# Maxima over partitions by a DMA transpose or by TensorE, in a fused local attention and feed-forward kernel

## Chip, core and metric

The kernel runs on one core of a Trainium2 chip. The metric is the device time of one execution in microseconds. Of three timed executions of the kernel before, the median was 618.79 us (614.6 to 619.58).

The engines are named as the profile names them: PE is TensorE's matmuls and PEld its weight loads, DVE is VectorE, ACT is ScalarE, POOL is GpSimd, and SP is the engine on whose queue this kernel issues all its DMAs. Each engine runs its instructions in the order in which they were recorded; one that waits holds back all behind it.

## What is computed

Attention over 4 batches, 8 heads, 768 positions and 64 channels, in which each position sees the keys less than 16 positions away and the 24 block summaries of its batch; then, on the same 3072 tokens of 512 channels, a feed-forward layer of width 2048. Cut from the reference:

```python
k_sum = k.reshape(B, H, nb, 32, D).max(axis=3)
v_sum = v.reshape(B, H, nb, 32, D).mean(axis=3)
scores_l = where(|i - j| < 16, scale * q @ k.T, -1e9)
scores_s = scale * q @ k_sum.T + log(32)
a = softmax(concat([scores_l, scores_s]))
x = a @ concat([v, v_sum])          # heads side by side: 3072 x 512
h = x @ w_in
out = (h * sigmoid(h)) @ w_out
```

## The kernel before, in words

**Precision sets the structure.** PE multiplies float16 here: a float32 operand is split into a high and a low half, and three products replace one. For that an operand is first scaled by a power of two, which is taken from the largest magnitude of the whole tensor. So before a batch's data can be split, a maximum (or a sum of magnitudes) that lies spread over the 128 partitions has to become one number that stands in every partition. `all_max` (L427) does that, eight times in the program: for the queries and keys of batches 1 to 3 (two columns, called by `job_scale`), for the values of batches 0 to 3 (one column, called by `v_scale`), and for the two weight matrices (two columns, called by `w_scale`). It writes the columns to DRAM (`sd`, L430), reads them back as one row spread to all partitions (`vms`, L431), and DVE reduces that row in each partition (L432). Five or six tiny DVE operations behind it make the scales (L441 to L446 for values: `sc`, `vsc`; L407 to L412 for queries and keys: `qc`, `qsc`; L813 to L817 for weights: `wc`, `ws`).

**Stages.** Batch 0 and the feed-forward of its first chunk of 256 tokens run in float32 (PE lines L626, L630, L688 and L727 for attention, L850 and L863 for the feed-forward) while the 16 MB of weights arrive (L771) and are decoded (ACT L785 and L789, DVE L791 and L792; the last gives the column maxima `wm`, and L810 reduces them to `wx`). Once `ws` is known, the weights are split in place (ACT L805, DVE L807). From there the feed-forward of the chunks 1 to 11 runs in float16, with L853 and L866 as its first and second product up to chunk 5, and L941 and L980 (fewer products, by sums of quarters) from chunk 6. The attention of the batches 1 to 3 is woven in two chunks ahead of its use: scores on PE (L623), a minimum with mask on DVE (L659), the exponential on ACT (L662), the split of the probabilities on DVE (L706) and their transposition by DMA (L709), then the product with the values (L742). Values of a batch need their scale before they are split (ACT L561, DVE L563) and written to DRAM. The three staging buffers `raw` are shared by all loads; `vR` is a transposed copy of the values that is loaded for their means and maxima (DVE L460, L462).

**What sets the order.** Nobody wrote the order by hand. The class `Plan` holds every operation with the engines it may run on, an assumed cost, its reads and writes by key and a priority. It places the operations on the engines by assumed times and latencies, forwards and backwards several times, and then records the instructions in order of their planned start. The assumed cost is the number in `plan.op({"dve": 140}, ...)`; an assumed DMA latency is added. The priorities contain the constants of the table `TUNE`. For `all_max` the plan assumes 600 and 450 ns for the two DMAs, beside their latencies. The plan also puts in idle matmuls (L337) where PE has nothing to do at the beginning.

Of the kernel before, what the change touches and what calls it, by code (L numbers as in the profile page):

```python
# [10 lines left out]
F32 = mybir.dt.float32  # L11
F32R = mybir.dt.float32r
F16 = mybir.dt.float16
U32 = mybir.dt.uint32
U16 = mybir.dt.uint16
AF = mybir.ActivationFunctionType
ALU = mybir.AluOpType
# [215 lines left out]
def local_attn_ffn(ctx: ExitStack, tc: tile.TileContext, qkT, qP, qF, kF, v, vR, vP, w, out):  # L233
# [23 lines left out]
    ident = const.tile([P, P], F32, name="ident")  # L257
    make_identity(nc, ident)

    sums = const.tile([P, BLK + 4 * NTILE - 4], F32, name="sums")  # L260
# [44 lines left out]
    md_t = [far.tile([NB, 2, DM], F16, name=f"md{i}") for i in range(B - 1)]  # L305
    sd_t = [far.tile([P, 2], F32, name=f"sd{i}") for i in range(2 * B)]
    vmf_t = const.tile([P, 4, P], F16, name="vmf")
# [27 lines left out]

    unit = ident.bitcast(mybir.dt.bfloat16)
    plan = Plan(tc, lambda: nc.tensor.matmul(out=bank[0][:, :2 * P], lhsT=unit[:, :P], rhs=unit, start=True, stop=True))  # L337
# [88 lines left out]

    def all_max(out, in_, r, w, prio):  # L427
        i, n = nxt("sd", 2 * B), in_.shape[1]
        flat, row = sd_t[i].rearrange("p n -> (p n)")[:n * P], vms_t[:, :n * P]
        plan.op({"dma": 600}, lambda e: nc.sync.dma_start(out=flat.rearrange("(p n) -> p n", n=n), in_=in_), r=r, w=[("sd", i)], prio=prio)  # L430
        plan.op({"dma": 450}, lambda e: nc.sync.dma_start(out=row, in_=flat.unsqueeze(0).to_broadcast([P, n * P])), r=[("sd", i)], w=[("vms", 0)], prio=prio)  # L431
        plan.op({"dve": 65 + 133 * n}, lambda e: nc.vector.tensor_reduce(out=out, in_=row.rearrange("q (p n) -> q n p", n=n), axis=AX.X, op=ALU.max), r=[("vms", 0)], w=w, prio=prio, port=())  # L432

# [3 lines left out]
    def v_scale(b, prio):  # L437
        vs = vsc_t[b % 2]
        all_max(sc2[:, 0:1], am_t[:, 7:8], ["am4"], ["sc2"], prio)
        steps = (  # L440
# [368 lines left out]
    def w_scale(prio):  # L809
        plan.op({"dve": 80}, lambda e: nc.vector.tensor_reduce(out=wx_t, in_=wm_t, axis=AX.X, op=ALU.max), r=[("wm", f, kind) for f in range(NFT) for kind in range(2)], w=["wx"], prio=prio)  # L810
        all_max(wc[:, 0:2], wx_t, ["wx"], ["wc"], prio)
        steps = (
            lambda e: nc.vector.tensor_scalar(out=wc[:, 2:4], in0=wc[:, 0:2], scalar1=1e-30, scalar2=None, op0=ALU.max),  # L813
            lambda e: nc.vector.tensor_scalar(out=wc[:, 0:2].bitcast(U32), in0=wc[:, 2:4].bitcast(U32), scalar1=0x7F800000, scalar2=None, op0=ALU.bitwise_and),
            lambda e: nc.vector.tensor_scalar(out=ws_t[:, 2:4], in0=wc[:, 0:2], scalar1=2.0 ** -12, scalar2=None, op0=ALU.mult),
            lambda e: nc.vector.reciprocal(out=ws_t[:, 0:2], in_=ws_t[:, 2:4]),
            lambda e: nc.vector.scalar_tensor_tensor(out=ws_t[:, 3:4], in0=ws_t[:, 2:3], scalar=1.0 / SHRINK, in1=ws_t[:, 3:4], op0=ALU.mult, op1=ALU.mult))  # L817
        for i, step in enumerate(steps):
            plan.op({"dve": 70}, step, w=["wc"] + (["ws"] if i > 1 else []), prio=prio)
# [348 lines left out]

TUNE = dict(quad=-30.75, vd=-11.0, ws=-845.5, s0=3027.0, wp=623.75, wm=55.75, km=703.75, w_dma=27.5, w_dec=-2.75, a0=490.0, a1=-2168.0, d1=201.25, span=75.25, post=3599.25, ffn2=753.0, jc0=-1061.5, jc1=716.0, jx0=-191.25, jx1=1364.5, vs=765.0, qk=-243.25, k=-423.0, v=1879.25, v0=-41.25, out=1280.75, first=65.75)

# [60 lines left out]
```

## Time and profile before

| | before |
|---|---|
| median of three executions | 618.79 us |
| profiled execution, its own time | 619.0 us |
| its span, first to last instruction | 617.2 us |
| mean granted clock of PE | 0.977 |
| PE busy | 580.0 us, 94% |
| PEld busy | 440.7 us, 71% |
| DVE busy | 470.3 us, 76% |
| ACT busy | 369.8 us, 60% |
| POOL busy | 170.4 us, 28% |
| HBM traffic | 119 GB/s over the span |

How to read it: the profile comes from one execution, whose own time is 619.0 us; the span is 1.8 us less. Busy times are the share in which an engine had an instruction under way. A granted clock of 1.00 is PE's 2.4 GHz, and 0.50 is 1.2 GHz; a stretch between them has had both.

### The profile page before, as it was taken

What the parts mean: (1) busy time and instruction counts of PE and PEld (TensorE: products, weight loads), DVE (VectorE), ACT (ScalarE), POOL (GpSimd) and SP (SyncE); (2) the same over time, 40 slices, a digit from 0 to 9 for tenths busy, and PEclk for the clock granted to TensorE, in tenths of its full rate; (3) what the DMA queues carried; (4) which work ended last, traced back from release to release, by engine and by line L of the source; (5) the groups of instructions that cost most, each with busy time, mean ns of one, the idle gap of its engine ahead of it and who ended that gap; (6) DMA issues with size and microseconds to landing.
All of it is one profiled execution on the core that took longest, in us unless ns stands there. A gap on an engine that the chain in (4) does not pass through costs nothing.

```text
span 617.2 us, 15861 instructions
## 1 busy us (share of the span) xinstructions
PE 580.0 (94%) x6235; PEld 440.7 (71%) x6235; DVE 470.3 (76%) x1244; ACT 369.8 (60%) x906; POOL 170.4 (28%) x318
## 2 busy tenths in 40 slices
PE   8988988996899998896999999999899999999997
PEld 5765645664566765563667688888688888888885
DVE  6986869885969585985789765886887988665655
ACT  4886929952847662843767674653567566544332
POOL 4230103200111022313322122452444554442220
PEclk9998999999899999897999999999799999999999
DMA  8998734331586666545665566244473722220001
GB/s 323 418 329 296 294 74 154 96 97 55 140 233 177 179 150 70 148 96 106 181 202 143 129 126 109 83 139 66 100 217 70 164 78 43 44 70 2 35 1 36
DMA packets 67698, 84.42 MB, mean 137 GB/s; under 512 B 44887, under 2 KB 46311, under 8 KB 65831
## 3 DMA queue, kind: packets, MB, share of 16 engines
q1 hardware_dynamic: 67622, 83.41, 49.1%
q8 instruction: 49, 0.80, 0.6%
q14 instruction: 27, 0.21, 0.2%
HBM read 62.39 MB, written 11.16 MB: 119 GB/s over the span
## 4 chain that ended last, share of the span: by engine, by line
PE 50%; DMA 27%; DVE 15%; ACT 5%; issue 2%; POOL 0%; SPq 0%; DVEq 0%; ACTq 0%
PE bank L941 15%; PE bank L980 13%; PE bank L866 9%; PE bank L853 8%; DMA sd<-am 7%; DMA vms<-sd 5%; DMA wr<-in_w_dram 3%; DMA raw<-in_vR_dram 2%; DMA wr<-in_v_dram 2%; PE bank L742 2%; DMA out_dram<-raw 2%; DVE e L659 1%; PE bank L623 1%; DMA sd<-qm 1%; DVE wr L807 1%
## 5 line engine op out<-in xcount | busy, mean ns | idle before, releaser
L941 PE MATMUL bank<-x,wr 128*128 128x256 f16 x1152 | 134.8, 273 | 0.0
L965 POOL TENSOR_TENSOR wr<-wr 128x128 f32<-128x128 f32 x160 | 88.2, 568 | 146.8 <-DVE wr L957 67.1
L941 PEld LDWEIGHTS <-wr 128*128 128x128 f16 x1152 | 112.5, 98 | 14.4
L980 PE MATMUL bank<-wr 128*128 128x256 f16 x987 | 119.3, 276 | 3.6 <-DVE sc L442 2.0
L853 PE MATMUL bank<-x,wr 128*128 128x256 f16 x960 | 112.2, 273 | 0.0
L980 PEld LDWEIGHTS <-wr 128*128 128x128 f16 x987 | 96.5, 99 | 17.2 <-DVE sc L442 2.3
L853 PEld LDWEIGHTS <-wr 128*128 128x128 f16 x960 | 93.7, 98 | 19.8 <-issue 0.9
L866 PE MATMUL bank<-wr 128*128 128x512 f16 x384 | 93.3, 390 | 9.3 <-DVE sc L441 4.9
L662 ACT ACTIVATE e<-e,mx 128x120 f32<-128x120 f32 x192 | 73.0, 382 | 26.1 <-DVE mx L659 23.7
L866 PEld LDWEIGHTS <-wr 128*128 128x128 f16 x384 | 36.9, 100 | 49.7 <-DVE sc L441 5.4
L675 POOL TENSOR_SCALAR first<-e,sum 128x120 f16<-128x120 f32 x54 | 24.5, 464 | 120.8 <-ACT e L662 29.4
L956 ACT ACTIVATE wr<-bank,th 128x512 f32<-128x512 f32 x47 | 32.0, 682 | 36.6 <-PE bank L941 36.4
L957 DVE SCALAR_TENSOR_TENSOR wr<-wr,bank 128x512 f32<-128x512 f32 x47 | 32.0, 682 | 27.3 <-ACT wr L956 27.3
L706 DVE SCALAR_TENSOR_TENSOR first<-e,sum,first 128x120 f16<-128x120 f32 x144 | 46.5, 375 | 0.0
L968 DVE SCALAR_TENSOR_TENSOR wr<-wr 128x512 f16<-128x512 f32 x47 | 33.7, 716 | 16.6 <-ACT wr L967 16.5
L967 ACT ACTIVATE wr<-wr 128x512 f16<-128x512 f32 x47 | 29.3, 623 | 26.4 <-POOL wr L965 26.3
L878 ACT ACTIVATE wr<-bank,th 128x512 f32<-128x512 f32 x32 | 21.8, 681 | 34.5 <-PE bank L853 34.3
L659 DVE CUSTOM_DVE_ANT_0 e<-bank,masks,qsc 128x120 f32<-128x120 f32 x144 | 41.1, 334 | 1.6 <-PE bank L623 1.6
L961 ACT ACTIVATE wr<-wr 128x384 f16<-128x384 f32 x47 | 24.4, 520 | 28.7 <-DVE wr L957 28.5
L246 POOL TENSOR_TENSOR wr<-wr 128x256 f32<-128x256 f32 x32 | 26.5, 846 | 36.9 <-DVE wr L926 30.7
L662 ACT ACTIVATION_READ_ACCUMULATOR e<-e,mx 128x1 f32 x192 | 36.1, 188 | 0.0
L962 DVE SCALAR_TENSOR_TENSOR wr<-wr 128x384 f16<-128x384 f32 x47 | 31.1, 662 | 4.7 <-ACT wr L961 3.8
(155 smaller groups left out, 861.5 us busy)
## 6 DMA issues: line engine op xcount, KB each, us to landing
wr<-in_w_dram SPq DMA_DIRECT2D x14, 1024.0 KB
raw<-in_qkT_dram SPq DMA_DIRECT2D x18, 576.0 KB
out_dram<-raw SPq DMA_DIRECT2D x23, 256.0 KB
first<-vd SPq DMA_DIRECT2D x30, 192.0 KB
raw<-in_kF_dram SPq DMA_DIRECT2D x12, 384.0 KB
raw<-in_qF_dram SPq DMA_DIRECT2D x9, 512.0 KB
raw<-in_vR_dram SPq DMA_DIRECT2D x12, 384.0 KB
raw<-in_vP_dram SPq DMA_DIRECT2D x9, 512.0 KB
```

The source lines that it names most:

```text
L659: plan.op({"dve": 262 if b else 206}, lambda e, i=i, j=j, et=et, mx=mx: nc.vector.tensor_tensor_reduce(out=et[:, i, :], in0=sc[j][:, i, :N ...
L662: plan.op({"act": 385}, lambda e, i=i, j=j, et=et, mx=mx: nc.scalar.activation(out=et[:, i, :], in_=et[:, i, :], func=AF.Exp, scale=-1.0, ...
L706: nc.vector.scalar_tensor_tensor(out=pt[:, i, P:P + NKEY], in0=et[:, i, :], scalar=su4[:, 2 * j + i:2 * j + i + 1], in1=pt[:, i, :NKEY], o ...
L853: nc.tensor.matmul(out=o, lhsT=wip[:, part, ct * P:(ct + 1) * P], rhs=x[:, ct, :], start=(ct == 0 and q == 0), stop=(ct == NCT - 1 and q = ...
L866: nc.tensor.matmul(out=bank[ob[u]][:, cs], lhsT=g[:, rows], rhs=wop[:, part, cs], start=(begins and q == 0), stop=(stops and q == 2))
L941: nc.tensor.matmul(out=h[:, at * CH:at * CH + CH], lhsT=wip[:, p, ct * P:(ct + 1) * P], rhs=x[:, ct, :], start=(ct == 0 and q == 0), stop= ...
L956: plan.op({"act": 573}, lambda e: nc.scalar.activation(out=t, in_=h, func=AF.Tanh, scale=th[:, 0:1]), r=bk(k) + [("th", b % 2), "areas"], ...
L957: plan.op({"dve": 604}, lambda e: nc.vector.scalar_tensor_tensor(out=t, in0=t, scalar=1.0, in1=h, op0=ALU.add, op1=ALU.mult), r=bk(k), w=t ...
L962: plan.op({"dve": 470}, lambda e: nc.vector.scalar_tensor_tensor(out=ld, in0=src, scalar=SHRINK, in1=hd, op0=ALU.mult, op1=ALU.subtract), ...
L965: plan.op({"pool": 470, "dve": 210}, lambda e, m=m, x=x, y=y, op=op: eng[e].tensor_tensor(out=sm[:, m], in0=x, in1=y, op=op), r=tks, w=[(" ...
L968: plan.op({"dve": 610}, lambda e: nc.vector.scalar_tensor_tensor(out=ls, in0=sf, scalar=SHRINK, in1=hs, op0=ALU.mult, op1=ALU.subtract), r ...
L980: nc.tensor.matmul(out=acc_of(c, m)[0], lhsT=x[:, left[m]], rhs=right[m](p), start=(opens and q == 0 and m in (1, 4, 2, 7)), stop=(closes ...
```

## The change

`all_max` gets two new forms, and the form over DRAM goes away together with its buffers `sd`.

For the queries, keys and values of the batches 1 to 3, DVE reads only the upper 16 bits of each float32, as bfloat16, and spreads each partition's value over 128 columns (L448, a copy inside `vms`). One DMA transpose turns that block (L449), so that every partition then holds all 128 values in a row, and DVE reduces them (L450). The scales use the exponent alone, which the upper 16 bits hold.

For the values of batch 0 and for the weights (`near`), PE transposes the column or columns to one row in PSUM (L438), DVE reduces the row on one partition (L441), a matmul with a row of ones spreads the result to 128 partitions (L442), and DVE copies it out of PSUM (L443).

The table `TUNE` is replaced as a whole, so priorities change everywhere and the plan orders all engines anew. The arithmetic of everything else is what it was. Lines after L257 move by 4, and lines behind `all_max` by 18: L741 to L760 in the new kernel are L723 to L742 in the old.

```diff
+    ones = const.tile([1, P], F32, name="ones")
+    nc.vector.memset(ones, 1.0)
+    row_t = const.tile([1, 2], F32, name="row")
...
-    sd_t = [far.tile([P, 2], F32, name=f"sd{i}") for i in range(2 * B)]
...
-    def all_max(out, in_, r, w, prio):
-        i, n = nxt("sd", 2 * B), in_.shape[1]
-        flat, row = sd_t[i].rearrange("p n -> (p n)")[:n * P], vms_t[:, :n * P]
-        plan.op({"dma": 600}, lambda e: nc.sync.dma_start(out=flat.rearrange("(p n) -> p n", n=n), in_=in_), r=r, w=[("sd", i)], prio=prio)
-        plan.op({"dma": 450}, lambda e: nc.sync.dma_start(out=row, in_=flat.unsqueeze(0).to_broadcast([P, n * P])), r=[("sd", i)], w=[("vms", 0)], prio=prio)
-        plan.op({"dve": 65 + 133 * n}, lambda e: nc.vector.tensor_reduce(out=out, in_=row.rearrange("q (p n) -> q n p", n=n), axis=AX.X, op=ALU.max), r=[("vms", 0)], w=w, prio=prio, port=())
+    def all_max(out, in_, r, w, prio, near=False):
+        n = in_.shape[1]
+        if near:
+            k = sbank()
+            row, spread = row_t[:, :n], bank[k][:, 2 * P:2 * P + n]
+
+            def turn(e):
+                for j in range(n):
+                    nc.tensor.transpose(out=bank[k][:1, j * P:(j + 1) * P], in_=in_[:, j:j + 1], identity=ident)
+
+            plan.op({"pe": 110 * n}, turn, r=r, w=bk(k), prio=prio, cols=128 * n)
+            plan.op({"dve": 65 + 133 * n}, lambda e: nc.vector.tensor_reduce(out=row, in_=bank[k][:1, :n * P].rearrange("o (a p) -> o a p", a=n), axis=AX.X, op=ALU.max), r=bk(k), w=["row"], prio=prio)
+            plan.op({"pe": 110}, lambda e: nc.tensor.matmul(out=spread, lhsT=ones, rhs=row, start=True, stop=True), r=["row"], w=bk(k), prio=prio, cols=1)
+            plan.op({"dve": 67}, lambda e: nc.vector.tensor_copy(out=out, in_=spread), r=bk(k), w=w, prio=prio)
+            return
+        top = in_.bitcast(BF16).rearrange("p (n i) -> p n i", i=2)[:, :, 1:].to_broadcast([P, n, P])
+        two = vms_t.bitcast(BF16)
+        here, there = (two[:, i * DM:i * DM + n * P].rearrange("p (n q) -> p n q", n=n) for i in range(2))
+        plan.op({"dve": 65 + 133 * n}, lambda e: nc.vector.tensor_copy(out=here, in_=top), r=r, w=[("vms", 0)], prio=prio)
+        plan.op({"dma": 1290}, lambda e: nc.sync.dma_start_transpose(out=there, in_=here.rearrange("p n q -> p (n q)")), r=[("vms", 0)], w=["tops"], prio=prio)
+        plan.op({"dve": 65 + 133 * n}, lambda e: nc.vector.tensor_reduce(out=out, in_=there, axis=AX.X, op=ALU.max), r=["tops"], w=w, prio=prio, port=())
...
-        all_max(sc2[:, 0:1], am_t[:, 7:8], ["am4"], ["sc2"], prio)
+        all_max(sc2[:, 0:1], am_t[:, 7:8], ["am4"], ["sc2"], prio, b == 0)
...
-        all_max(wc[:, 0:2], wx_t, ["wx"], ["wc"], prio)
+        all_max(wc[:, 0:2], wx_t, ["wx"], ["wc"], prio, True)
...
-TUNE = dict(quad=-30.75, vd=-11.0, ws=-845.5, s0=3027.0, wp=623.75, wm=55.75, km=703.75, w_dma=27.5, w_dec=-2.75, a0=490.0, a1=-2168.0, d1=201.25, span=75.25, post=3599.25, ffn2=753.0, jc0=-1061.5, jc1=716.0, jx0=-191.25, jx1=1364.5, vs=765.0, qk=-243.25, k=-423.0, v=1879.25, v0=-41.25, out=1280.75, first=65.75)
+TUNE = dict(quad=-1617.75, vd=-16.25, ws=-11.25, s0=-8.0, wp=1561.25, wm=184.25, km=10.25, w_dma=-1358.75, w_dec=-8.0, a0=-982.0, a1=-827.75, d1=698.0, span=86.25, post=3268.5, ffn2=759.5, jc0=-207.25, jc1=-485.5, jx0=-32.75, jx1=2269.75, vs=1653.25, qk=572.0, k=-650.75, v=1762.5, v0=301.75, out=-105.5, first=53.0)
```

How the order moves is shown at three places. The first is SP's queue while the weights are loaded and the scale of batch 0's values is made (`am` is the column of maxima, `in_w` the weights, `in_v` values, `in_qP` queries). In the kernel before:

```order
L527 DMA wr<-in_v_dram 128x1024 x2
L771 DMA wr<-in_w_dram 128x2048
L430 DMA sd_135<-am 128x1
L771 DMA wr<-in_w_dram 128x2048
L431 DMA vms<-sd_135 128x128
L486 DMA second<-in_qP_dram 128x512
L771 DMA wr<-in_w_dram 128x2048 x6
```

And SP's queue at that place in the changed kernel:

```order
L789 DMA wr<-in_w_dram 128x1024 x3
L789 DMA wr<-in_w_dram 128x2048 x6
L504 DMA second<-in_qP_dram 128x512
L789 DMA wr<-in_w_dram 128x2048 x4
L545 DMA wr<-in_v_dram 128x1024 x2
L789 DMA wr<-in_w_dram 128x2048 x3
```

The two DMAs of the maximum are gone from between the weight loads. The second place is DVE at the scale of batch 1's values, ahead of and behind the reduction that ends the round trip. In the kernel before:

```order
L760 SCALAR_TENSOR_TENSOR x_183<-bank_188,vsc_157,x_183 128x4x128
L497 SCALAR_TENSOR_TENSOR second<-raw_118,qsc_150,second 128x512
L882 SCALAR_TENSOR_TENSOR work<-work 128x512
L500 SCALAR_TENSOR_TENSOR second<-raw_118,qsc_150,second 128x4x160
L807 SCALAR_TENSOR_TENSOR wr<-wr,ws 128x2x512
L460 TENSOR_REDUCE vm<-raw_120 128x24
L659 ISA e_175,mx_169<-bank_191,masks,qsc_150 128x120
L659 ISA mx_169 128x1
L432 TENSOR_REDUCE sc_156<-vms 128x1
L879 SCALAR_TENSOR_TENSOR work<-work,bank_186 128x512
L659 ISA e_175,mx_169<-bank_191,masks,qsc_150 128x120
L659 ISA mx_169 128x1
```

And DVE there in the changed kernel:

```order
L448 COPY vms<-am 128x128
L518 SCALAR_TENSOR_TENSOR second<-raw_121,qsc_145,second 128x4x160
L778 SCALAR_TENSOR_TENSOR x_178<-bank_183,vsc_152,x_178 128x4x128
L478 TENSOR_REDUCE vm<-raw_123 128x24
L897 SCALAR_TENSOR_TENSOR work<-work,bank_181 128x512
L450 TENSOR_REDUCE sc_151<-vms 128x1
L900 SCALAR_TENSOR_TENSOR work<-work 128x512
L459 TENSOR_SCALAR sc_151<-sc_151 128x1
L677 ISA e_170,mx_164<-bank_186,masks,qsc_145 128x120
L677 ISA mx_164 128x1
```

Four operations now stand between the copy that starts the exchange and the reduction that ends it. The third place is SP's queue around the same scale (`in_vR` are the values for the maxima, `in_vP` those to be split). In the kernel before:

```order
L459 DMA raw_120<-in_vR_dram 128x768
L494 DMA raw_118<-in_qkT_dram 128x1152
L430 DMA sd_138<-am 128x1
L431 DMA vms<-sd_138 128x128
L560 DMA raw_118<-in_vP_dram 128x1024
L560 DMA raw_120<-in_vP_dram 128x1024
```

And in the changed kernel:

```order
L449 DMA_TRANSPOSE vms<-vms 128x2x128
L477 DMA raw_121<-in_vR_dram 128x768
L512 DMA raw_121<-in_qkT_dram 128x1152
L477 DMA raw_123<-in_vR_dram 128x768
L449 DMA_TRANSPOSE vms<-vms 128x1x128
L578 DMA raw_121<-in_vP_dram 128x1024
L578 DMA raw_123<-in_vP_dram 128x1024
```

The transposes stand where the pairs stood, and the loads of `in_vP` still follow; the transpose for the queries and keys is here too, with two of the four loads of `in_vR` behind it.

## Rows read from the trace of the kernel before

**Rows 1.** The page's first part: busy time, share of the span, instructions.
```profile
PE 580.0 (94%) x6235; PEld 440.7 (71%) x6235; DVE 470.3 (76%) x1244; ACT 369.8 (60%) x906; POOL 170.4 (28%) x318
```

**Rows 2.** PE's waits: line, whom it waited for, us in total, times, longest.
```profile
PE bank L623 <- DVE mx L659: 6.9, 2, 6.7
PE bank L866 <- DVE sc L441: 4.9, 1, 4.9
PE bank L866 <- ACT wr L881: 4.4, 1, 4.4
PE bank L626 <- DVE sc L441: 2.2, 1, 2.2
PE bank L980 <- DVE sc L442: 2.0, 1, 2.0
```

**Rows 3.** Timeline of DVE: start, us, operation, idle before and its end.
```profile
153.48 0.29 DVE L432 TENSOR_REDUCE sc<-vms 128x1 f32<-128x128 f32 x1 [7.04 <-DMA vms<-sd]
283.37 0.28 DVE L432 TENSOR_REDUCE sc<-vms 128x1 f32<-128x128 f32 x1 [8.44 <-DMA vms<-sd]
433.50 0.29 DVE L432 TENSOR_REDUCE sc<-vms 128x1 f32<-128x128 f32 x1 [6.84 <-DMA vms<-sd]
```

**Rows 4.** The chain that ended last, in order of time: start, us, what.
```profile
81.89 4.52 DMA sd<-wx
86.43 4.18 DMA vms<-sd
...
269.17 8.45 DMA sd<-am
277.64 5.71 DMA vms<-sd
```

**Rows 5.** Stretches: us, busy PE, PEld, DVE, ACT, POOL, PE's granted clock, DMA share, GB/s.
```profile
40.00:47.00 7.00, 5.35 (x23) 3.16 (x21) 4.93 (x11) 5.02 (x12) 2.46 (x6) 1.00 0.72 189
47.00:52.00 5.00, 3.38 (x12) 1.82 (x10) 1.09 (x2) 3.00 (x5) 0.00 (x0) 1.00 0.78 82
50.00:60.00 10.00, 7.78 (x82) 5.30 (x81) 7.81 (x29) 5.20 (x10) 0.00 (x0) 0.83 1.01 374
80.00:95.00 15.00, 13.04 (x97) 7.26 (x96) 9.50 (x19) 5.83 (x10) 0.00 (x0) 1.00 0.47 122
150.00:160.00 10.00, 3.93 (x56) 2.27 (x57) 6.20 (x31) 5.61 (x20) 1.57 (x4) 0.66 0.28 111
280.00:290.00 10.00, 5.68 (x22) 2.72 (x23) 6.21 (x22) 3.85 (x6) 2.55 (x6) 0.66 0.55 129
430.00:440.00 10.00, 7.32 (x49) 5.08 (x48) 5.91 (x25) 5.75 (x13) 3.77 (x8) 0.78 0.23 71
```

**Rows 6.** SP's timeline: two DMA transposes, and the store that waits for each.
```profile
289.80 1.22 SPq L470 DMA_TRANSPOSE vmp<-vmf  x1
...
294.67 1.15 SPq L474 DMA_DIRECT2D md<-vmp  x2
...
438.32 1.20 SPq L470 DMA_TRANSPOSE vmp<-vmf  x1
...
440.92 0.90 SPq L474 DMA_DIRECT2D md<-vmp  x2
```

**Rows 7.** DVE's groups by form: count, busy us, mean ns, idle before.
```profile
L500 DVE SCALAR_TENSOR_TENSOR second<-raw,qsc,second 128x640 f16<-128x640 f32 x18 | 16.2, 901 | 0.0
L760 DVE SCALAR_TENSOR_TENSOR x<-bank,vsc,x 128x512 f16<-128x512 f32 x4 | 3.0, 739 | 0.0
L460 DVE TENSOR_REDUCE vm<-raw 128x24 f32<-128x768 f32 x12 | 11.3, 943 | 0.0
L879 DVE SCALAR_TENSOR_TENSOR work<-work,bank 128x512 f32<-128x512 f32 x15 | 10.2, 679 | 3.3 <-ACT work L878 3.3
```

**Rows 8.** Timeline: a load of `vR` on SP, and the reduction that waited for it.
```profile
232.89 0.36 SPq L459 DMA_DIRECT2D raw<-in_vR_dram  x1
...
243.77 0.95 DVE L462 TENSOR_REDUCE am<-raw 128x1 f32<-128x768 f32 x1 [6.65 <-DMA raw<-in_vR_dram]
```

More of the change, by code (lines that the diff above doesn't have):

```diff
@@ L13 @@
 F16 = mybir.dt.float16
+BF16 = mybir.dt.bfloat16
 U32 = mybir.dt.uint32
@@ L334, in local_attn_ffn @@
     bank = [psum.tile([P, 512], F32, name=f"bank{i}") for i in range(8)]
-    unit = ident.bitcast(mybir.dt.bfloat16)
+    unit = ident.bitcast(BF16)
     plan = Plan(tc, lambda: nc.tensor.matmul(out=bank[0][:, :2 * P], lhsT=unit[:, :P], rhs=unit, start=True, stop=True))
```

## The prediction

> **What bounds the kernel now.** I read the page's first part before anything else: PE is busy for 580.0 of 617.2 us, every other engine for 76% or less [rows 1]. So PE's work is the floor, and a change that adds next to nothing to that work can gain at most the 37.2 us in which PE stands idle, and what a lower clock costs behind a stand. The second view is the list of PE's waits [rows 2]: it shows for whom PE stands. Four of its five longest lead to the place where this change works. L441 and L442 are the tiny operations that turn a maximum into a scale, and L659 (`mx`), for which L623 waits 6.9 us, follows the reduction L432 on DVE. The third view, DVE's timeline, says why: L432 stood 7.04, 8.44 and 6.84 us at the scales of the values of batches 1, 2 and 3 because `vms` had not arrived [rows 3], and DVE runs in order, so all work behind it stood too. The fourth view, the chain, gives the round trip itself: 8.45 us to write 128 numbers and 5.71 to read them back at batch 2, 4.52 and 4.18 for the weights [rows 4]. The DMA engines are 28% busy around 150 us and 23% around 430 [rows 5], so this is latency and not lack of bandwidth. The fifth view, stretches, shows the price on PE. At 150 to 160 it is busy for 3.93 us at a granted clock of 0.66, at 280 to 290 for 5.68 at 0.66, at 430 to 440 for 7.32 at 0.78 [rows 5]: after a stand part of the work runs at 1.2 instead of 2.4 GHz, so such a stand costs more than its length.
>
> **Values of batches 1 to 3: the gain.** If DVE no longer stands, PE gets back its wait and the clock behind it. Clock: busy time times one minus the granted clock, 3.93 x 0.34 = 1.3, 5.68 x 0.34 = 1.9, 7.32 x 0.22 = 1.6 us [rows 5]. Waits: 6.9 and 4.9 us by the list [rows 2]; for batch 3 the whole idle time of the stretch, 10.00 - 7.32 = 2.7 [rows 5], 2.0 of which the list names. That is 8.2, 6.8 and 4.3, together **19.3 us**. It is kept to the end only if PE stays the bound between the gaps, which its 94% speaks for.
>
> **Their new cost.** The exchange is now copy, transpose, reduction. Before shows no such transpose of one column, but it has two others: the store that waits for L470 is issued 4.87 us after it at 289.80 and 2.60 us after it at 438.32 [rows 6], so a small transpose is here to be used 2.6 to 4.9 us after its issue (four tiles there, one or two here). What covers it at batch 1 is the DVE work that the new order puts between copy and reduction: L518, L778, L478 and L897, which are L500, L760, L460 and L879 of before: 0.90 + 0.74 + 0.94 + 0.68 = 3.3 us [rows 7]. So DVE stands 0 to 1.6 us, and I take **0.7**, between the two. At batches 2 and 3 I take nothing: DVE stood 8.44 and 6.84 us there and PE only 4.9 and 2.0 [rows 2, 3], so PE has 3.5 to 4.8 us of stock that covers the same remainder; without that cover it is 1.6 us each. The six copies added on DVE are at most like the reductions of 128 columns, 0.28 or 0.29 us [rows 3], and twice that for two columns: three of each make 2.6 us. DVE is 76% busy, so some fill gaps; from 0 to 2.6 I take **0.5**. On SP 16 small DMAs go, 6 transposes of about 1.2 us of issue [rows 6] come. Each holds back the loads queued behind it until the copy is done, above all those of `in_vR` and `in_vP`; I price that among the rivals.
>
> **Batch 0.** In SP's queue the read-back L431 waits for `sd` with seven weight loads and a load of queries behind it, as the order shows. The load stream falls from 374 GB/s (50 to 60) to 189 at 40 to 47 and 82 at 47 to 52 [rows 5]. In stream time that is 7 x (374 - 189)/374 + 5 x (374 - 82)/374 = 3.5 + 3.9 = 7.4 us. By the new order nothing there waits for DVE. But what PE does in this phase hangs on decoding by ACT and DVE too. PE's idle time there is 1.65, 1.62 and 2.22 us in the three stretches (50 to 52 counted twice), and the clock 7.78 x 0.17 = 1.3 [rows 5], so the gain lies between 0 and 6.8; I take **4**, since 2.2 us of it are the wait for this very scale [rows 2] and the stream is the likeliest cause of most of the rest.
>
> **Weights.** The round trip of 4.52 + 4.18 = 8.7 us [rows 4] becomes two transposes, a reduction, a matmul and a copy. Five steps of 0.3 us or so (L432's row again) with PE and DVE each free only after what is under way there (0.3 to 1.3 us) come to 2 to 4 us, so `ws` is known about 5 to 6 us sooner. PE is idle 15.00 - 13.04 = 2.0 us around it [rows 5]; that is the most that comes straight back, and as the lead is over twice as long I take **2** of 0 to 2. What PE does in the new path is five tiny instructions; the danger is that the in-order PE stands until DVE has made the row. Twice 0 to 2 us gives 0 to 4; most of that is hidden if the plan puts other DVE work behind and not ahead, and I take **1**.
>
> **The new order.** `TUNE` changes everything else. The before order has one accident that is not an exchange: L462 on DVE waited 6.65 us for a `vR` load issued at 232.89 [rows 8], and PE then 4.4 for ACT behind it [rows 2]. Such a thing can vanish or come, so -6 to +6 us, and I take **0**.
>
> **Sum.** 19.3 + 4 + 2 = 25.3 gained; 0.7 + 0.5 + 1 = 2.2 lost; net 23. The profiled execution took 619.0 us, its span 617.2, and the median is 618.8, so the two agree: 619.0 - 23 = **596 us**.
>
> **Rivals.**
> *The first phase does not yield* (20%). Batch 0, the weights and the stand at batch 1 lie in the phase where ACT and DVE decode and split weights: DVE and ACT are busy 7.81 and 5.20 us of 10 at 50 to 60 [rows 5]. If PE is short of split weights or of `mx` anyway, the 6.9 us at L623 only move to another producer. Then batches 2 and 3 alone remain, 6.8 + 4.3 = 11.1: 608 us, 604 to 612. Against it: DVE stood idle for all of the 7.04 us [rows 3], and an engine that is idle is not the bound.
> *More than the sum* (10%). The wait for the `vR` load goes too and the first phase gives all: another 4.4 + about 1.5 of clock, and 2.8 at batch 0, so 585 to 589.
> *The exchange is not shorter* (12%). If a transpose lands as late as the `vR` load of [rows 8], 243.77 - 232.89 = 10.9 us after its issue, DVE stands as long as now: 10.9 - 3.3 = 7.6 at batch 1 against 7.04. Then only batch 0 and the weights can give, 613 to 625. Against it: that load is 128 x 768 float32, some 390 KB, beside others, and a transpose here 32 or 64 KB. A page would make the round trip cheap from the start: the Trainium skill, "DMA: Bandwidth & Descriptors", section "Anatomy of one DMA", has about 2 us of fixed cost for each DMA, most of it the receipt of the write, in a fit for DMAs issued from GpSimd. By that rule the pair would cost about 4 us and the one transpose 2, and three exchanges would save 6 us in all: an estimate of 613 from that page. The trace disagrees: here the pair takes 8.45 + 5.71 us at batch 2 [rows 4], on SP's queue.
> *Slower* (8%). Each of the six transposes waits at the head of SP's queue for a DVE copy; the loads of `in_vR` and `in_qkT` behind it start late, and an operation of DVE waits for them as L462 did. One such event cost PE 4.4 us [rows 2], with the clock about 6. The net gain of 23 is used up by four events; with all six it is 619 - 23 + 36 = 632, and from five on it is over 625. Against it: before had sixteen DMAs that waited in the same queue, two for each exchange, and just one such event.
>
> **How the numbers follow.** The forecast has 50% and reaches from 589 (batch 0 and the order at their better ends by half) to 604 (batch 0, weights nothing, the transpose 1.6 late). The range, 585 to 612, takes in the first three cases whole, 0.5 + 0.2 + 0.1 = 8 in 10, and leaves out the fourth and the fifth. About 1%, 6 us, is what a measurement of this kernel can tell from no change. Faster by more than that, below 612.8, are the first three cases: 0.5 + 0.2 + 0.1 = 0.8. Within it the fourth, 0.12; slower the last, 0.08.
>
> **What would show it.** Right: DVE stands under 1.6 us ahead of L450 three times; PE's list of waits has no entry of over 2 us that leads to a scale's tiny operations or to `mx`; the granted clock near the three scales is 0.9 or more; SP's stream at 40 to 52 us is near 374 GB/s; `ws` follows `wx` in 2 to 4 us; PE's busy time is still about 580 us less the clock's share. Wrong: L450 standing 5 us or more (the exchange), or PE as idle as before around 40 to 160 us with another producer named (the first phase), or `vR` loads issued late behind a transpose (the queue). The sum itself would be wrong if PE's idle total falls by the 15 to 20 us named and the span does not.

## The result, and the profile after

The changed kernel takes **580.8 us** (median of 4, 580.4 to 582.1) beside 618.8 for the kernel before in the same series: ratio 0.940, 95% interval 0.936 to 0.945. The prediction said 596, 585 to 612: the direction was right, the gain of 38 us is far more than the 23 forecast, and the time lies below the range. In the later series the kernel before read 614.7 to 615.6 us and the changed one 581.9 (ratio 0.945, 0.941 to 0.948), so beside the experiments the gain is 34 us. The profiled executions, with spans of 617.2 and 580.4 us, differ by 36.8.

The changed kernel's busy times:

```profile
PE 569.9 (98%) x6238; PEld 437.9 (75%) x6238; DVE 474.1 (82%) x1260; ACT 362.8 (63%) x897; POOL 171.5 (30%) x320
```

PE does the same number of matmuls within three as before [rows 1], in 10.1 us less busy time, and is idle 10.5 us in place of 37.2. Its longest waits in the changed kernel (line, whom it waited for, us in total, times, longest):

```profile
PE bank L881 <- DVE work L897: 1.4, 1, 1.4
PE bank L340 <- POOL ident masks.py:199: 1.4, 1, 1.4
PE bank L644 <- DVE mx L677: 1.2, 2, 0.6
PE bank L745 <- ACT third L240: 1.1, 1, 1.1
```

Nothing over 1.4 us is left, and all five entries of [rows 2] are gone. DVE's reductions behind the transpose, at the values of batches 1, 2 and 3 (start, us, operation, idle before in brackets):

```profile
136.22 0.28 DVE L450 TENSOR_REDUCE sc<-vms 128x1 f32<-128x128 bf16 x1
...
254.57 0.27 DVE L450 TENSOR_REDUCE sc<-vms 128x1 f32<-128x128 bf16 x1
...
393.29 0.29 DVE L450 TENSOR_REDUCE sc<-vms 128x1 f32<-128x128 bf16 x1 [1.46 <-DMA vms<-vms]
```

Where [rows 3] show stands of 7.04, 8.44 and 6.84 us there are 0, 0 and 1.46. Of SP, the transposes ahead of the first and the third of them:

```profile
133.42 1.13 SPq L449 DMA_TRANSPOSE vms<-vms  x1
...
388.37 1.12 SPq L449 DMA_TRANSPOSE vms<-vms  x1
```

The first was here within 2.8 us of its issue, since L450 did not wait at 136.22; the third took 4.9. These are the two ends of [rows 6].

The weights, in the changed kernel (wx to ws):

```profile
76.20 0.19 DVE L828 TENSOR_REDUCE wx<-wm 128x2 f32<-128x32 f32 x1
...
79.28 0.16 DVE L443 COPY wc<-bank 128x2 f32<-128x2 f32 x1 [0.76 <-PE bank L442]
...
80.28 0.16 DVE L835 SCALAR_TENSOR_TENSOR ws<-ws 128x1 f32<-128x1 f32 x1
```

From `wx` to `wc` it is 3.2 us, where the pair of DMAs alone took 8.7 [rows 4]. And the stretch in which the stream of weights ran dry before, in the columns of [rows 5]:

```profile
40.00:47.00 7.00, 7.00 (x28) 4.41 (x27) 7.00 (x11) 6.96 (x11) 1.73 (x5) 1.00 1.01 418
47.00:52.00 5.00, 5.00 (x78) 3.31 (x77) 5.00 (x8) 4.49 (x6) 2.48 (x3) 1.00 1.03 422
```

418 and 422 GB/s in place of 189 and 82, with PE busy throughout. The two stretches are the same in time and not in place: the new order has made batch 0's exchange by 25.5 us already, where in the kernel before L431 still held SP's queue until 46.90. What the exchange costs in one and the same order is tried below.

### The profile page after: what moved, and what is told of

The parts are those of the page before. It is cut to its first block, busy times and chain, and to the rows that moved or that the text cites. A ratio compares the mean times of both kernels' runs of the same rounds, so it can differ in the third digit from the quotient of the medians.

```text
span 580.4 us, 15857 instructions
## 1 busy us (share of the span) xinstructions
PE 569.9 (98%) x6238; PEld 437.9 (75%) x6238; DVE 474.1 (82%) x1260; ACT 362.8 (63%) x897; POOL 171.5 (30%) x320
## 4 chain that ended last, share of the span: by engine, by line
PE 71%; DVE 14%; DMA 7%; ACT 4%; issue 2%; SPq 0%; DVEq 0%; POOL 0%; ACTq 0%; POOLq 0%
PE bank L959 22%; PE bank L998 19%; PE bank L871 11%; PE bank L884 11%; PE bank L760 2%; DVE e L677 2%; PE bank L641 2%; DMA raw<-in_qF_dram 2%; DVE wr L809 2%; DMA raw<-in_qkT_dram 1%; DVE first L724 1%; DVE wr L900 1%; DMA first<-in_kF_dram 1%; DVE wr L897 1%; DMA raw<-in_kF_dram 1%
## 5 line engine op out<-in xcount | busy, mean ns | idle before, releaser
L983 POOL TENSOR_TENSOR wr<-wr 128x128 f32<-128x128 f32 x157 | 84.9, 557 | 139.8 <-DVE wr L975 57.3
L998 PE MATMUL bank<-wr 128*128 128x256 f16 x987 | 115.7, 273 | 0.0
L884 PE MATMUL bank<-wr 128*128 128x512 f16 x384 | 89.8, 380 | 1.0 <-DVE am L453 0.6
L974 ACT ACTIVATE wr<-bank,th 128x512 f32<-128x512 f32 x47 | 32.0, 682 | 40.4 <-PE bank L959 40.2
L693 POOL TENSOR_SCALAR first<-e,sum 128x120 f16<-128x120 f32 x50 | 25.5, 519 | 105.7 <-DVE sum L686 34.5
L724 DVE SCALAR_TENSOR_TENSOR first<-e,sum,first 128x120 f16<-128x120 f32 x144 | 48.4, 388 | 0.0
L985 ACT ACTIVATE wr<-wr 128x512 f16<-128x512 f32 x47 | 29.3, 623 | 28.6 <-POOL wr L983 27.8
L986 DVE SCALAR_TENSOR_TENSOR wr<-wr 128x512 f16<-128x512 f32 x47 | 33.0, 702 | 12.8 <-ACT wr L985 12.8
L899 ACT ACTIVATE wr<-wr 128x512 f16<-128x512 f32 x32 | 20.0, 626 | 26.1 <-DVE wr L897 26.1
L693 POOL TENSOR_SCALAR e<-e,sum 128x120 f32<-128x120 f32 x31 | 11.3, 381 | 80.4 <-DVE mx L677 47.7
```

Of the source, the lines that this page charges most:

```text
L693: nc.gpsimd.tensor_scalar(out=out, in0=src, scalar1=by, scalar2=0.0, op0=ALU.mult, op1=ALU.add)
L724: nc.vector.scalar_tensor_tensor(out=pt[:, i, P:P + NKEY], in0=et[:, i, :], scalar=su4[:, 2 * j + i:2 * j + i + 1], in1=pt[:, i, :NKEY], o ...
L884: nc.tensor.matmul(out=bank[ob[u]][:, cs], lhsT=g[:, rows], rhs=wop[:, part, cs], start=(begins and q == 0), stop=(stops and q == 2))
L974: plan.op({"act": 573}, lambda e: nc.scalar.activation(out=t, in_=h, func=AF.Tanh, scale=th[:, 0:1]), r=bk(k) + [("th", b % 2), "areas"], ...
L983: plan.op({"pool": 470, "dve": 210}, lambda e, m=m, x=x, y=y, op=op: eng[e].tensor_tensor(out=sm[:, m], in0=x, in1=y, op=op), r=tks, w=[(" ...
L986: plan.op({"dve": 610}, lambda e: nc.vector.scalar_tensor_tensor(out=ls, in0=sf, scalar=SHRINK, in1=hs, op0=ALU.mult, op1=ALU.subtract), r ...
```

## Where the 36.8 us were

The whole span in two stretches, before and then after (same columns):

```profile
0.00:125.00 125.00, 112.23 (x1033) 76.76 (x1035) 100.16 (x256) 94.78 (x218) 26.96 (x64) 0.99 0.71 247
125.00:617.00 492.00, 467.77 (x5209) 363.93 (x5204) 370.16 (x988) 274.98 (x689) 143.45 (x254) 0.98 0.45 109
```

```profile
0.00:125.00 125.00, 119.31 (x1069) 82.09 (x1070) 111.10 (x275) 97.94 (x218) 26.51 (x71) 1.00 0.67 251
125.00:580.00 455.00, 450.57 (x5171) 355.83 (x5169) 363.00 (x985) 264.89 (x680) 144.96 (x249) 1.00 0.51 115
```

PE's idle time fell from 12.8 to 5.7 us up to 125 us, and from 24.2 to 4.4 behind it; together 26.9. The remaining 10 us are the lower busy time. They are the clock. These stretches of the kernel before hold most of its idle time:

```profile
40.00:60.00 20.00, 15.84 (x113) 10.27 (x112) 13.83 (x41) 12.15 (x23) 2.46 (x6) 0.91 0.85 257
100.00:120.00 20.00, 17.79 (x178) 12.44 (x179) 17.34 (x40) 19.93 (x50) 9.96 (x15) 1.00 0.40 127
140.00:160.00 20.00, 13.06 (x167) 8.72 (x165) 12.57 (x43) 8.88 (x27) 2.58 (x6) 0.83 0.16 57
240.00:260.00 20.00, 15.65 (x140) 9.65 (x138) 16.23 (x49) 11.46 (x32) 5.28 (x8) 0.91 0.36 95
280.00:300.00 20.00, 15.68 (x134) 9.48 (x135) 13.30 (x36) 8.13 (x13) 5.44 (x10) 0.83 0.54 140
420.00:440.00 20.00, 17.32 (x211) 13.87 (x200) 12.56 (x45) 11.06 (x30) 8.34 (x16) 0.89 0.36 68
```

And these run from the moment at which PE works again, behind each of the five waits of [rows 2], until its clock is full again:

```profile
52.90:57.00 4.10, 4.10 (x67) 2.92 (x68) 4.10 (x8) 1.73 (x2) 0.00 (x0) 0.58 1.03 434
155.80:160.00 4.20, 3.92 (x56) 2.25 (x57) 3.87 (x17) 4.20 (x15) 1.57 (x4) 0.60 0.00 0
248.50:252.00 3.50, 3.50 (x10) 1.12 (x11) 3.50 (x21) 3.49 (x13) 0.01 (x1) 0.60 0.62 114
284.40:290.00 5.60, 5.60 (x22) 2.63 (x23) 5.18 (x19) 3.85 (x6) 2.55 (x6) 0.60 0.26 71
434.90:443.00 8.10, 7.43 (x39) 4.95 (x40) 7.10 (x21) 6.67 (x13) 5.22 (x10) 0.58 0.19 38
```

Busy time times one minus the granted clock is 1.7, 1.6, 1.4, 2.2 and 3.1: 10.0 us. In the changed kernel's profile the mean granted clock is 1.00. So each of these five waits was paid for twice, once as idle time and once as work at 1.2 GHz behind it, and the second part was over a quarter of the gain. The shorter stands at 100 to 120 us cost no clock. How much clock a kernel loses differs between its executions: of the kernel before one took 611.2 us at a mean granted clock of 0.988 and another 617.6 at 0.978, and the profile, at 0.977, is one of the costlier.

## The experiments

**The exchange or the new order?** The plan makes its order from assumed costs, not from the instruction that is issued. So an exchange can be swapped while every other instruction keeps its place: the kernels of this group differ from their parent by the exchanges' own instructions alone.

The kernel before with six new exchanges (e4_far_new_old_order): at the places where the pair was recorded, the copy and the transpose.

```diff
-    def all_max(out, in_, r, w, prio):
+    def all_max(out, in_, r, w, prio, near=False):
...
-        plan.op({"dma": 600}, lambda e: nc.sync.dma_start(out=flat...), ...
-        plan.op({"dma": 450}, lambda e: nc.sync.dma_start(out=row...), ...
+        plan.op({"dma": 600}, lambda e: nc.sync.dma_start(out=flat...) if near else nc.vector.tensor_copy(out=here, in_=top), ...
+        plan.op({"dma": 450}, lambda e: nc.sync.dma_start(out=row...) if near else nc.sync.dma_start_transpose(out=there, ...), ...
```

> The kernel before with its order kept; only the six exchanges for queries, keys and values of batches 1 to 3 are copy, transpose and reduction. Theory 'the exchange': the 19.3 us of the prediction less about 2 for a wait of some 3 us that little covers there: about 601 us, 597 to 605. Rival 'the order': over 610.

Measured 592.2 us beside 614.7 (ratio 0.963, 0.960 to 0.966): a gain of 22.5, where the theory had some 17 (from 618.8 to 601) and the rival under 9; the time lies below the range of both.

The changed kernel with the same six over DRAM (e1_far_dram, the first piece), with the other two (e2_near_dram, the second piece; what is read back lies in `vmp`, which is not in use so early), and with all eight (e3_all_dram, both):

```diff
-        plan.op({"dve": 65 + 133 * n}, lambda e: nc.vector.tensor_copy(out=here, in_=top), ...
-        plan.op({"dma": 1290}, lambda e: nc.sync.dma_start_transpose(out=there, ...), ...
+        plan.op({"dve": 65 + 133 * n}, lambda e: nc.sync.dma_start(out=flat..., in_=in_), ...
+        plan.op({"dma": 1290}, lambda e: nc.sync.dma_start(out=line, in_=flat.unsqueeze(0)...), ...
...
-            plan.op({"pe": 110 * n}, turn, ...
-            plan.op({"dve": 65 + 133 * n}, lambda e: nc.vector.tensor_reduce(out=row, ...), ...
-            plan.op({"pe": 110}, lambda e: nc.tensor.matmul(out=spread, ...), ...
-            plan.op({"dve": 67}, lambda e: nc.vector.tensor_copy(out=out, in_=spread), ...
+            plan.op({"pe": 110 * n}, lambda e: nc.sync.dma_start(out=flat..., in_=in_), ...
+            plan.op({"dve": 65 + 133 * n}, lambda e: nc.sync.dma_start(out=line, ...), ...
+            plan.op({"pe": 110}, lambda e: None, ...
+            plan.op({"dve": 67}, lambda e: nc.vector.tensor_reduce(out=out, in_=line...), ...
```

> The changed kernel with its order kept instruction for instruction; only the six exchanges for queries, keys and values of batches 1 to 3 go over DRAM again (write where the copy stood, read-back where the transpose stood). Theory 'the exchange' (the time went out of the round trips): the pair takes about 14 us at each scale of values and the order covers about 3.3, so DVE stands some 10 us three times; less 3.5 to 4.8 us of stock on PE, plus 1.3 to 1.9 us of clock, about 8 each: 581 + 24 = 605 us, 600 to 612. Rival 'the order' (the new table gains most, by a place for the scales where nothing waits): 583 to 590 us.

> The changed kernel with its order kept; only the two exchanges by TensorE (values of batch 0, weights) go over DRAM again, six exchanges stay transposes. Theory 'the exchange': SP's queue stands again for the write with eleven weight loads behind it and the weights' scale comes 6 us later: the 4 and 2 us of the prediction, up to 8: 587 us, 584 to 590. Rival 'the order': 580 to 583.

> The changed kernel with its order kept and all eight exchanges over DRAM: what the new order is worth with the old exchange. Theory 'the exchange': the losses of the two kernels before it add up, about 611 us, 605 to 619. Rival 'the order': at most 592.

Measured 612.6, 602.9 and 633.0 us beside 614.7. Against the 580.8 or 581.9 of the changed kernel the six cost 31 to 32 us in this order, the two 21 to 22, and all eight 51 to 52, nearly the sum of both. With the old exchange the new order is even 3% slower than the kernel before (1.030, 1.027 to 1.034). So with its order kept the new table is no gain of its own, and the rival falls. All three lie above the ranges of the theory, e1_far_dram by 0.6 us. DVE in e1_far_dram at the three scales of values:

```profile
146.26 0.29 DVE L453 TENSOR_REDUCE sc<-vms 128x1 f32<-128x128 f32 x1 [9.27 <-DMA vms<-sd]
...
277.58 0.28 DVE L453 TENSOR_REDUCE sc<-vms 128x1 f32<-128x128 f32 x1 [9.04 <-DMA vms<-sd]
...
427.54 0.28 DVE L453 TENSOR_REDUCE sc<-vms 128x1 f32<-128x128 f32 x1 [8.67 <-DMA vms<-sd]
```

About 9 us each, near the 10 expected. What the expectation had at nothing are the queries and keys: at batch 2's, DVE stood 3.14 us for a load of `vR` and PE 2.71 behind it, at batch 3's DVE stood 2.77 us for the pair, and PE 3.33. In e2_near_dram the price was far above the expected 6. SP there at batch 0, then DVE and PE at batch 0 and at the weights:

```profile
21.35 0.33 SPq L443 DMA_DIRECT2D sd<-am  x1
28.33 0.33 SPq L444 DMA_DIRECT2D vmp<-sd  x1
28.70 3.97 SPq L792 DMA_DIRECT2D wr<-in_w_dram  x5
```

```profile
33.77 0.29 DVE L446 TENSOR_REDUCE sc<-vmp 128x1 f32<-128x128 f32 x1 [8.25 <-DMA vmp<-sd]
...
96.90 0.42 DVE L446 TENSOR_REDUCE wc<-vmp 128x2 f32<-128x256 f32 x1 [9.98 <-DMA vmp<-sd]
```

```profile
36.94 3.78 PE L884 MATMUL bank<-wr,work 128*128 128x512 f32 x4 [7.79 <-DVE work L900]
...
104.24 2.08 PE L884 MATMUL bank<-wr,work 128*128 128x512 f32 x2 [10.11 <-DVE work L900]
```

The read-back holds SP for 6.7 us with the weights behind it; in the kernel before it was 13.6, since there the write took 16.7 us, for a reason that was not tried. And DVE, which stands for the pair, holds back the work that PE needs, 7.8 us at batch 0 and 10.1 at the weights. (The stands of 10.1 and 7.8 us in the expectation of e10_batch0_dram below are these two, the first of them at the weights.) The 21 to 22 us are the price in an order planned for the short way by TensorE; the old order, planned for a pair, gives a smaller one below.

**The term of the new order: an accident, or the pair in SP's queue?** The prediction took DVE's 6.65 us at L462 [rows 8] for an accident of the order. The kernel before with only the three exchanges for queries and keys replaced, order kept (e13_only_qk_new_old_order; the edit of e4_far_new_old_order with the condition below):

```diff
-        ... if near else nc.vector.tensor_copy(out=here, in_=top)
+        ... if near or n == 1 else nc.vector.tensor_copy(out=here, in_=top)
```

> The kernel before with its order kept; only the three exchanges for queries and keys are copy, transpose and reduction, the values' and the weights' stay over DRAM. In the kernel before, L431 held SP's queue from 226.4 to 231.0 us at batch 2's queries and keys, with the load of vR behind it for which DVE stood 6.65 us and then PE 4.4 at L866. If the pair in SP's queue was the cause: that stand goes, with the clock behind it, 4.4 + 1 to 2: 608 to 610 us beside 614.8 of before. If it was an accident of the order: 613 to 615.

Measured 608.4 us beside 615.3 (ratio 0.989, 0.985 to 0.992). SP in the kernel before, and in this one:

```profile
226.00 0.33 SPq L430 DMA_DIRECT2D sd<-qm  x1
230.99 0.33 SPq L431 DMA_DIRECT2D vms<-sd  x1
```

```profile
226.84 1.17 SPq L436 DMA_TRANSPOSE vms<-vms  x1
228.92 0.67 SPq L597 DMA_DIRECT2D first<-vd  x2
232.19 0.36 SPq L464 DMA_DIRECT2D raw<-in_vR_dram  x1
```

The load of `vR` left 6.9 us after the write of the pair before [rows 8], and 5.4 after the transpose here. DVE's stand for that load, and PE's stretch:

```profile
239.40 0.95 DVE L467 TENSOR_REDUCE am<-raw 128x1 f32<-128x768 f32 x1 [3.85 <-DMA raw<-in_vR_dram]
```

```profile
240.00:260.00 20.00, 19.20 (x180) 13.36 (x179) 20.00 (x61) 14.12 (x35) 5.31 (x8) 1.00 0.52 123
```

DVE stood 3.85 us where it was 6.65, and PE is idle for 0.8 where it was 4.35, at a full clock. So this was the exchange as well, one step removed: not through the reduction L432, which waited 0.33 us here in the kernel before, but through the queue that the pair held. Only 1.5 us of it is the later issue, though. The load was also slower: from its issue to its use it took 10.9 us in the kernel before [rows 8] and takes 7.2 here. There the read-back and two loads of `vd` left within 1.9 us ahead of it, bunched behind the held queue; that they slowed it is likely, and was not tried by itself.

Nor is the gain all from this place, and that it fell into the range expected for it is in part luck. The two profiled spans differ by 9.1 us, of which 3.55 of idle time and 1.4 of clock are here. Batch 3 gave more (first the kernel before, then this one):

```profile
400.00:460.00 60.00, 56.38 (x684) 47.67 (x682) 48.14 (x125) 34.02 (x85) 27.03 (x50) 0.94 0.52 128
```

```profile
400.00:460.00 60.00, 58.38 (x767) 50.39 (x765) 46.05 (x123) 34.24 (x85) 26.83 (x50) 1.00 0.50 133
```

There 2.0 us of idle time and 3.1 of clock are gone. In the kernel before DVE had stood 2.9 us for batch 3's queries and keys, which it no longer does; whether that is the cause, or the difference in clock between executions, these runs do not tell. So the 6.9 us are the price of the three exchanges for queries and keys together.

**Is it TensorE that counts at batch 0 and the weights, or only to be off DRAM?** The kernel before, order kept, with all eight exchanges as transposes (e9_all_transposed_old_order, the condition of e4_far_new_old_order set to never):

```diff
-        dram = near
+        dram = False
```

> The kernel before with its order kept and all eight exchanges, batch 0's values and the weights too, as copy, DMA transpose and reduction. With six of eight it was 592.2 us. Theory 'the exchange': batch 0 and the weights give back the 4 and 2 us of the prediction or somewhat more, since 10 us of PE's idle time before 120 us stayed in the kernel with six: 584 to 588, within a few us of the changed kernel. Rival 'the order': these two exchanges give under 2 us in the old order and the last 11 us come from the new table: 590 to 593.

584.9 us beside 614.9 (0.952, 0.947 to 0.957), as expected: the two give 7.4 more. 30 of the 34 us are thus had in the old order, with no TensorE.

In the changed kernel's order, only batch 0 over DRAM (e10_batch0_dram), both of the two as transposes (e12_near_transposed), only the weights as a transpose (e14_weights_transposed), and the changed kernel beside it (after_again). e10_batch0_dram is the second piece above for batch 0 alone; the other two have copy, transpose and reduction in the same three places, e14_weights_transposed for the weights alone:

```diff
-            plan.op({"pe": 110 * n}, turn, ...
-            plan.op({"dve": 65 + 133 * n}, lambda e: nc.vector.tensor_reduce(out=row, ...), ...
...
+            plan.op({"pe": 110 * n}, lambda e: nc.vector.tensor_copy(out=here, in_=top), ...
+            plan.op({"dve": 65 + 133 * n}, lambda e: nc.sync.dma_start_transpose(out=there, ...), ...
```

> The changed kernel with its order kept; only the exchange for batch 0's values goes over DRAM, the weights' stays on TensorE. Both together cost 22.1 us in this order, and PE's two stands at L884 were 10.1 and 7.8. If each costs its own stand and the clock behind it: 580.8 + 12 = 593 us, 590 to 596. If batch 0's exchange only delays the weights, and the weights' scale is what counts: under 588.

> The changed kernel with its order kept; the two exchanges on TensorE (values of batch 0, weights) are copy, DMA transpose and reduction as well. If what counts is only to be off DRAM: 581 to 584 us, since a transpose is 2 to 3 us longer than the way by TensorE. If the transpose waiting in SP's queue holds back the weight loads, or 3 us at these two scales cost PE: 585 to 590.

> The changed kernel with its order kept; the weights' exchange is copy, DMA transpose and reduction, batch 0's values stay on TensorE. With both as transposes it was 585.2 us, DVE stood 2.9 us at the weights' reduction and 0.2 at batch 0's, and PE 2.9 at L883. If TensorE is worth its gain at the weights, where PE has nothing else split: 584 to 586. If it is batch 0's weight stream: under 582.5.

> The changed kernel itself, beside the kernels it is compared with, since the kernel before has read 618.8 us in one series and 615 in the others: 580 to 582 us. If it follows the kernel before: 577 to 579.

e10_batch0_dram took 591.7 us, as expected, with PE standing 8.7 us there: batch 0 costs 10 to 11 and the weights, by the difference to e2_near_dram, 11. e12_near_transposed took 585.2 (0.950, 0.945 to 0.955), above what "only off DRAM" allowed. DVE's waits there:

```profile
DVE wc L446 <- DMA vmp<-vmp: 2.9, 1, 2.9
...
DVE sc L446 <- DMA vmp<-vmp: 0.2, 1, 0.2
```

e14_weights_transposed took 582.8 and the changed kernel 581.9 in one series (0.946, 0.942 to 0.950, and 0.945, 0.941 to 0.948): no difference that can be told, and between the two expectations. So TensorE against a transpose is worth some 3 to 4 us for both together and at most 1 or so at the weights; that the rest lies at batch 0's stream is only what remains, it was not measured by itself, and it is near the limit of what is measured here. And with all eight as transposes the old and the new order are equal, 584.9 and 585.2.

| us | all over DRAM | six new, two DRAM | all transposed | six transposed, two on TensorE |
|---|---|---|---|---|
| old order | 614.7 | 592.2 | 584.9 | not tried with the order kept |
| new order | 633.0 | 602.9 | 585.2 | 580.8, 581.9 |

**Was the latency too long, or only not planned for?** These four are planned anew, so their order changes as well. The changed kernel with the old table (e5_new_max_old_table), the kernel before with the new one (e6_old_max_new_table): the `TUNE` lines exchanged. The kernel before with the pair's times of the trace in the plan (e7_true_cost_old_table), and the changed kernel with its six exchanges over DRAM and the same costs (e11_far_dram_true_cost):

```diff
-        plan.op({"dma": 600}, lambda e: nc.sync.dma_start(out=flat...
+        plan.op({"dma": 600 + 5500}, lambda e: nc.sync.dma_start(out=flat...
...
+        keep, plan.slack = plan.slack, dict(plan.slack, dve=4250)
         plan.op({"dve": 65 + 133 * n}, lambda e: nc.vector.tensor_reduce(out=out, in_=row...
+        plan.slack = keep
```

> The changed kernel with the old table of constants, planned anew with the new exchanges. Theory 'the exchange': 581 to 587 us. Rival 'the order': the new table is worth 8 us or more with the new exchanges: 589 or above.

> The kernel before with the new table of constants, planned anew with the old exchanges and their old assumed costs. Theory 'the exchange': the table is of no use without the new exchanges, 612 to 635 us. Rival 'the order': the table carries a gain of its own, 605 or below.

> The kernel before, exchanges over DRAM as they are, but the plan is told what they take in the trace: 5.5 us more for the write on SP and 4.25 us more until DVE may use what is read back; all is planned anew. Theory 'the latency was not planned for' (DVE stands because the plan put the reduction too early, not because there is no other work): 592 to 602 us. Rival 'the latency itself' (what follows a scale has no other work to hide behind): 610 or above.

> The changed kernel with its table, batch 0's values and the weights on TensorE; the six exchanges of batches 1 to 3 go over DRAM, and the plan is told what they take in the trace (5.5 us more for the write on SP, 4.25 more until DVE may use what is read back) and orders all anew. With its order kept, this exchange made it 612.6 us. Theory 'the latency was not planned for': a latency of 14 us that is planned has other work to hide behind in these batches: 582 to 592 us. Rival 'the latency itself': 600 or above.

588.4 us for e5_new_max_old_table, between the two expectations: planned anew with the old table, some 7 us stay behind, though with the order kept the old order lost nothing. So much the new table may be worth as a fit to the new costs. 629.5 for e6_old_max_new_table (1.021, 1.015 to 1.027): the new table with the old exchange loses, planned anew or not. 591.6 for e11_far_dram_true_cost (0.961, 0.956 to 0.966), where the same six exchanges over DRAM cost 612.6 with the order kept. Its second stretch, and its exchange at batch 2's values (SP, then DVE):

```profile
125.00:589.00 464.00, 457.84 (x5213) 360.21 (x5210) 368.11 (x993) 276.57 (x702) 131.10 (x234) 1.00 0.46 115
```

```profile
256.49 0.33 SPq L448 DMA_DIRECT2D sd<-am  x1
263.85 0.34 SPq L449 DMA_DIRECT2D vms<-sd  x1
```

```profile
271.37 0.28 DVE L451 TENSOR_REDUCE sc<-vms 128x1 f32<-128x128 f32 x1
```

The write still held SP for 7.4 us and 14.9 us pass until L451, but the plan had put other work there: no idle time before it, and PE idle for 6.2 us in the stretch against 24.2 in the kernel before. So at batches 1 to 3 the round trip hurt because the plan took it for shorter than it is. (The same kernel planned anew with the old costs was not tried, so what planning anew does by itself is not known.) e7_true_cost_old_table came to 607.5 (0.988, 0.982 to 0.993), between its two expectations. There too DVE waits at none of the reductions, yet it shows where that does not help. Its stretches around the weights' scale, and DVE there:

```profile
90.00:100.00 10.00, 7.33 (x74) 3.47 (x72) 2.41 (x3) 1.19 (x2) 0.00 (x0) 0.83 0.32 105
100.00:110.00 10.00, 5.43 (x82) 3.84 (x77) 7.53 (x33) 7.94 (x26) 4.00 (x9) 0.65 0.33 96
```

```profile
100.28 0.28 DVE L661 CUSTOM_DVE_ANT_0 e<-bank,masks 128x120 f32<-128x120 f32 x1 [7.54 <-PE bank L632]
...
104.06 0.39 DVE L433 TENSOR_REDUCE wc<-vms 128x2 f32<-128x256 f32 x1
```

DVE is busy for 2.41 us of 10 and ACT for 1.19 before the scale is there. The plan put work ahead of the reduction that itself waited, 7.54 us for PE, and the reduction came at 104.06 where the kernel before had it at 90.63. So this order found little to do between `wx` and `ws`; that none could is not shown. What else makes up the 10 us between e11_far_dram_true_cost and the changed kernel, with another order throughout, stays open.

## Why the prediction was wrong

Its mechanism held: the round trips made DVE stand, PE behind it, the clock behind PE, and all of that went. The expected sum of 23 missed 14 of the 37 us, term by term:

- **Values of batches 1 to 3, idle time: right.** 14.5 us were forecast. By the stretches of 20 us above it was 6.94 + 4.32 + 2.68 = 13.9, and the changed kernel is idle for 0.6 us around batch 2's scale and for nothing around the others. Measured alone, from e13_only_qk_new_old_order to e4_far_new_old_order, the three are worth 16.2 with clock and costs; the forecast for them was 19.3 - 1.2 = 18.1.
- **The clock: too small.** 4.8 us were taken at these three scales, with a clock averaged over 10 us in which PE also stood, and at batch 3 over a stretch that ended while the clock was still low. Over PE's work until the clock's return it is 1.6, 2.2 and 3.1, 6.9 us, and 10.1 in the whole kernel by PE's busy time.
- **The new order, taken as 0 with bounds of 6: the step that failed outright.** The "one accident that is not an exchange" came from an exchange. The row of SP ahead of the load was never read: L431 stood in the queue from 226.4 to 231.0, waiting for the write. 4.35 us of idle time and 1.4 of clock hung on it, and 3.6 and 1.4 of them went in e13_only_qk_new_old_order. The sum has no term for the exchanges of the queries and keys, which that run puts at 6.9 us for all three. The rival "more than the sum" had this wait going, for no reason given, and put 585 to 589 on it at 10%; the result lies below that too.
- **Batch 0 and the weights: too small.** 4 + 2 - 1 were taken. In the old order, as transposes, they gave 7.4; idle time up to 125 us fell by 7.1 and 1.7 of clock went behind batch 0's scale. The cap of 2 us at the weights was set by the 2.0 us around the scale. PE's 2.2 us at 100 to 120 went too, but they were 0.7 in e13_only_qk_new_old_order, which has the weights' exchange over DRAM, so they are not shown to be its price. The feared 1 us for PE in the new path is not in its list of waits.
- **Costs of the new exchange: none to be seen.** DVE stood 1.46 us once, at batch 3, and PE did not wait for it.
- **The new table: its 0 was right for the wrong reason.** With the orders kept it is worth nothing with transposes (584.9 and 585.2), and costs 18 us with DRAM (614.7 and 633.0); planned anew, the old table is 7 us behind (588.4).

Two slips changed no term of the sum: behind L431 the order shows six weight loads, not seven, and half of 2.8 (batch 0) and half of 6 (the order) take 596 to 592, not to the forecast's lower end of 589.

Of the rivals, "the first phase does not yield" falls: PE's idle time up to 125 us went from 12.8 to 5.7, and the 6.94 at 140 to 160 to nothing. "The exchange is not shorter" falls: in the kernel before the pair took 8.4 to 14.2 us, and 22 at batch 0, against 2.8 to 5.3 for a transpose for which DVE waited. The Trainium skill, "DMA: Bandwidth & Descriptors", section "Anatomy of one DMA", has some 2 us of fixed cost for each DMA in a fit for DMAs issued from GpSimd; the pairs on SP's queue whose end these runs show took 7.1 us or more, and the 6 us that the rule gave for the change are a sixth of what it brought. "Slower" falls too: the transposes do hold SP, and less than the pairs did. Part of the miss is the base, whose profile lost much to the clock: taken from the 615 of the later series, the forecast gain of 23 gives 592, 10 us above their 581.9, where it is 15 on record.

## What to carry to other kernels

A late load in a list of waits is not a cause: go back to its issue, and to what stood in that queue ahead of it, before calling it an accident; a small DMA that waits for another DMA on an in-order queue delays strangers. Count what a lower clock costs over the work alone, from the end of the stand to where the clock is full again. And before shortening a latency, see whether the plan that made the order knows it: where other work existed, planning anew with the true length gave 21 of 31 us back (612.6 to 591.6); at the weights it found little, and only the shorter way was seen to help.

## What was unexpected of the hardware

The write of a column of 128 single numbers to DRAM took 6.9 to 8.9 us in the chains of these kernels at batches 1 to 3 (8.45 in [rows 4]); that of two columns, in pieces twice as long, took 4.1 to 5.8 (4.52 there), and in e13_only_qk_new_old_order the weights' write was over within 2.8. Twice the bytes in less time was seen in each kernel in which both stand in the chain; why was not tried. At batch 0, amid the stream of weights, the single column took 16.7 us in the kernel before and 7.0 in e2_near_dram.
